# PSUM laid out by engine, seven-row x tiles and one DMA transpose per unit in a fused convolution and expert layer

## The chip, the cores and the metric

The kernel runs on one core of a Trainium2 chip. The metric is the device time of one execution in microseconds, lower is better. Five engines have instruction streams of their own: TensorE (PE, with its weight loads as PEld), VectorE (DVE), ScalarE (ACT), GpSimd (POOL) and SyncE (SP). SP issues most of the DMAs, in the order of its program, and POOL those that scatter rows.

## The reference

For each of 8 batches of 3584 tokens with 192 channels, a causal convolution over 7 taps with weights of its own for every token and head (a softmax over the taps), and then a top-1 layer of 8 experts on all 28672 tokens:

```python
w = softmax(weight_gen)                          # B, S, 8 heads, 7 taps
out = np.einsum('bshk,bskhg->bshg', w, x_unf)    # x_unf: the token and the 6 before it
x = out.reshape(28672, 192)
e_idx = np.argmax(x @ w_gate, axis=1)
gate_w = softmax(x @ w_gate)[e_idx]
eom = sigmoid(x @ w_output_gate)
h = relu(x[mask] @ w1[e])                        # w1: 8 x 192 x 1024
out[mask] = gate_w * eom[e] * (h @ w2[e])        # w2: 8 x 1024 x 192
```

## The kernel before

**Units.** The tokens are cut into 32 units of 896, four to a batch. In a unit a partition holds 7 consecutive tokens (`JS` = 7), so a tile of 7 rows has 7 x 192 = 1344 columns. The causal taps need the 6 rows before (the halo), so an `x` tile holds 13 rows, 2496 columns. `x_load` loads all 13 from DRAM for a unit that is not the first of its batch (24 of the 32); the first of a batch gets zeros from ACT (`zero_steps`) in place of rows before its start.

**The convolution of a unit.** `softmax_steps` makes the tap weights. DVE's share of them, `tw`, goes to PSUM; there are several places for it, among them 3904 and 1344, which lie in banks into which PE writes sums. `tap_steps` then multiplies rows by weights, four or five of the seven taps on POOL (tile `gap`), the rest on DVE. For the first 6 units (`PE_U`) PE adds the products with identity matmuls in f32; from unit 6 on DVE adds them in PSUM (`acc_steps`).

**From sums to tokens in DRAM.** `sum_steps` scales a unit's sum on ACT and splits it into high and low f16 halves on DVE (tile `rt`). The gate needs these rows with channels on partitions (tile `gt`). For units 0 to 4, `pe_logits` turns two rows at a time: six transposes on PE into one place of PSUM, `turn`, then one ACT copy of 128 x 768 (the seventh row alone, 128 x 384), four rounds per unit. From unit 5 on (`TR_U`) SP issues seven DMA transposes per unit, each of three blocks of 128 x 128 f16, 189 in all. Then come logits on PE, softmax, argmax and ranks on DVE, and POOL scatters the rows to their expert's places in `srtd` in DRAM (7 scatters per unit).

**Experts.** In the front, `weight_steps` and `split_steps` load, scale and split the 8 experts' weights and write them to `wd` in DRAM; the sum of squares from which the scale comes is reduced by a matmul in the place that the turned rows use. Tiles of up to 512 tokens of one expert are then formed in rounds. For a tile SP reads its number, then loads `meta`, `xT` (a DMA transpose from `srtd`), `wa` and `wb`; PE runs GEMM1, ACT makes `hh` and DVE `hl` from it (high and low halves), PE runs GEMM2, ACT scales it to `ys`, and POOL scatters it out. The first tile is loaded after the eighth expert has been written.

**Order.** No instruction's place is decided at run time. While the kernel is built, generators ("chains") yield the engine on which they want to issue next, and a planner (`Order`, `Paced` for engines, `Queue` for SP) with a model of costs (`LAT`, `ARRIVE`, `LEAD` and others) picks whose turn it is. A waiting instruction holds everything behind it on its engine. PE's writes and other engines' accesses to PSUM wait for each other by bank of 512 f32 columns, whichever columns of the bank are touched. The tiles are numbered in the order of their loads.

Of the kernel before, what the change touches and what calls it, by code (L numbers as in the profile page):

```python
# [9 lines left out]
F16 = mybir.dt.float16  # L10
# [8 lines left out]
W = 194  # L19
WW = 3585  # L20
# [63 lines left out]
class Order:  # L84


    def __init__(self):
        self.now, self.chains, self.port, self.ring = 0.0, [], 0.0, Ring()
        self.cur = Chain(None, (), 0.0, None)

    def add(self, gen, rank, engine, t=None):
        c = Chain(gen, rank, self.cur.t if t is None else t, engine)
        c.label = label(gen)
        c.favour = FAVOUR.get(c.label, 0.0)
        self.chains.append(c)
        return c

# [42 lines left out]
class Queue:  # L140
# [12 lines left out]
    def __getattr__(self, name):  # L153
        f = getattr(self.engine, name)

        def call(*args, **kwargs):
            c, own, issue = self.order.cur, self.cost(name, args, kwargs), self.issue(name, args, kwargs)
            r = f(*args, **kwargs)  # L158
            if self.host is not None:
                self.issued = max(self.host.t, c.t)  # L160
                self.host.t = self.issued + issue
            self.issued = max(self.issued, self.order.now) + issue
            if own is not None:
                done = self.order.ring.land(self.issued - issue + ARRIVE, own)
                self.moved = max(self.moved, done)
                c.t = max(c.t, done + LANDED)
            return r

        return call


class Paced:
# [8 lines left out]
    def __getattr__(self, name):  # L181
        f = getattr(self.engine, name)

        def call(*args, **kwargs):
            if self.first is not None:
                self.first(self.order.cur.t - self.t)
            c, own = self.order.cur, self.cost(name, args, kwargs)
            r = f(*args, **kwargs)  # L188
            if own is not None:
                held = LOCK and self.holds is not None and self.holds(kwargs)  # L190
# [63 lines left out]
def sync_issue(name, args, kwargs):  # L254
    return 1.29 if name == "dma_start_transpose" else 0.48
# [20 lines left out]
def kernel(ctx: ExitStack, tc: tile.TileContext, x, wg, wgate, wogate, w1, w2, cst, out):  # L276
# [58 lines left out]
    tr_free, lg_free, rk_free, tw_free = [0.0], [(0.0, 2048)], [(0.0, 2272), (0.0, 2288)], []  # L335
# [4 lines left out]
    turn = ps[:, 1536:1920].bitcast(F16)  # L340
# [17 lines left out]
    rest_free = [(0.0, 3904), (0.0, 1344)]  # L358
# [46 lines left out]
    zeros = cp.tile([1, D], F32, name="zeros")  # L405
    nc.gpsimd.memset(zeros, 0.0)
# [15 lines left out]
    for i in range(RT):  # L422
        rt_free.append((0.0, rp.tile([P, JS, W], I32, name=f"rt_{i}")))
# [7 lines left out]
    rr = cf[0:1, o : o + RMAX * 9].rearrange("p (a b) -> p a b", b=9)  # L431
    o += RMAX * 9
# [20 lines left out]
    nc.vector.tensor_copy(f_rr, rr[:, :, 0])  # L453
    pad = cp.tile([P, W], I32, name="pad")
    nc.gpsimd.memset(pad, 0)
    nc.gpsimd.memset(pad[:, 193:194], 65535)
# [58 lines left out]
    def gate_steps():  # L515
# [11 lines left out]
        pg = ps[:, 2304:2320]  # L527
# [34 lines left out]
    def split_steps(e, st1, st2):  # L562
# [7 lines left out]
        yield from take(tr_free, T_)  # L570
        pg = ps[:, 1536:1538]
# [4 lines left out]
        yield from scales(pg[:, 0:2], sc, inv, f"w{e}", tr_free)  # L576
# [37 lines left out]
    def load_steps():  # L614
        for u in range(1, NU):
# [7 lines left out]
            yield from take(x_free, SP)  # L623
            x_load(u)
# [12 lines left out]
    def softmax_steps(u):  # L637
# [20 lines left out]
        if u == PE_U - 1:  # L658
            yield V, lambda: rest_free or tw_free
        home = tw_free if u >= PE_U or (u == PE_U - 1 and not rest_free) else rest_free  # L660
        _, at = yield from take(home, V)
        tw = ps[:, at : at + NV * (K - n)].rearrange("p (v k) -> p v k", k=K - n)
        V.tensor_tensor(out=tw, in0=w4[:, :, n:K], in1=f_mx.unsqueeze(2).broadcast_to([P, NV, K - n]), op=ALU.mult)
        U[u]["tw"], U[u]["tw_at"], U[u]["tw_k"], U[u]["tw_home"] = tw, at, n, home
# [7 lines left out]
    def tap_steps(eng, tag):  # L672

        for u in range(NU):
# [4 lines left out]
            yield eng, lambda: "soft" in d and "zero" in d and (tag == "ga" or "split" in U[u - 2])  # L679
            od.cur.t = max(od.cur.t, d["wt"], d["xt"])  # L680
# [98 lines left out]

    def sum_steps(u):  # L780

        d = U[u]
        _, ri = yield from take(rt_free, S)
        d["ri"], rt = ri, ri.bitcast(F16)
# [22 lines left out]
        if u >= TR_U:  # L807
            yield from take(gt_free, TQ)
            gt = rp.tile([P, JS, 3, P], F16, tag="gt", bufs=GT, name=f"gt{u}")
            for j in range(JS):  # L810
                TQ.dma_start_transpose(out=gt[:, j], in_=rt[:, j, 0:384])
# [9 lines left out]
        else:  # L821
            od.cur.t += LAT_T
            for j0 in range(0, JS, 2):
                yield T_
                for j in range(j0, min(j0 + 2, JS)):
                    logits(lg, j, gt[:, j].rearrange("p k r -> p (k r)"))
            gt_free.append(od.cur.t)

        lz = d["lz"] = sp.tile([P, JS, 3, 8], F32, tag="lz", name=f"lz{u}")
# [10 lines left out]
        eq = sp.tile([P, JS, 8], F32, tag="eq", name=f"eq{u}")  # L840
        mb = m.unsqueeze(2).broadcast_to([P, JS, 8])
        V.tensor_tensor(out=l8, in0=l8, in1=mb, op=ALU.subtract)
        ex = d["ex"] = sp.tile([P, JS, 8], F32, tag="exl", name=f"exl{u}")
# [28 lines left out]
    def pe_logits(u, rt, lg):  # L872

        gx = None
        yield from take(gt_free, S)
        gt = rp.tile([P, JS, 3, P], F16, tag="gt", bufs=GT, name=f"gt{u}").rearrange("p j k r -> p j (k r)")
        for g0 in range(0, JS + 2, 2):
            for g in range(2):
                j = g0 - 2 + g
                if gx is not None and j < JS:  # L880
                    logits(lg, j, gt[:, j])
            ng = min(2, JS - g0)
            if ng > 0:
                yield from take(tr_free, T_)
                pt = turn
                for g in range(ng):
                    for k in range(3):
                        T_.transpose(out=pt[:, g * 384 + k * 128 : g * 384 + (k + 1) * 128], in_=rt[:, g0 + g, k * 128 : (k + 1) * 128], identity=ident)
                yield S
                gx = True  # L890
                S.copy(gt[:, g0 : g0 + ng, 0:384], pt[:, 0 : ng * 384].rearrange("p (j c) -> p j c", c=384))
                tr_free.append(od.cur.t)
                yield T_
        gt_free.append(od.cur.t)
        U[u]["turned"] = True

# [29 lines left out]
    def place_steps(u):  # L926
# [40 lines left out]
        rt_free.append((d["sent_t"], d["ri"]))  # L967
# [226 lines left out]
    def bank_steps():  # L1194
# [4 lines left out]
        yield T_, lambda: any(f[1] == 1344 for f in rest_free)  # L1199
        rest_free.remove(next(f for f in rest_free if f[1] == 1344))  # L1200
        bank_free.extend((got[0], 512 * i) for i in range(3))

    def last_sum_steps():
# [3 lines left out]
        acc_free.append(t)  # L1207
        yield T_, lambda: "all" in state
        bank_free.extend((od.cur.t, at) for at in (2560, 3072, 3584, 2048))

    def last_turn_steps():
# [8 lines left out]
        tw_free.append((t, 2048))  # L1220
# [87 lines left out]
    with tc.For_i(0, left, 1):  # L1308
        first_weights(wp, 1, "more")
        _, more = wa_free.pop()  # L1310
        for to, of in ((f_done, state["done"]), (f_rr, rr[:, :, 0])):
# [36 lines left out]
LAT = 0.118  # L1348
LAT_S = 0.191
LAT_P = 0.34  # L1350
LAT_T = 1.864
LOCK = True
ARRIVE = 1.3
LANDED = 0.8
LAT_R = 1.0
SLACK = 0.024
SCATTER = 0.987
SMALL = 0.066
EAGER = 0, 0.2, (2, 3, 4)
LEAD = 4.586  # L1360
# [15 lines left out]
SHARES = {4: 5, 5: 5, 8: 5, 13: 4, 31: 4}  # L1376
# [9 lines left out]
WBX = 5.532  # L1386
# [25 lines left out]
```

## Time and profile before

| | |
|---|---|
| median of three runs | 1239.97 us (1239.14 to 1242.26) |
| the profiled execution | 1237.59 us, of it 1235.8 us span |
| busy: PE, PEld | 1126.0 us (91%), 816.4 us (66%) |
| busy: DVE, ACT, POOL | 941.5 us (76%), 588.4 us (48%), 834.4 us (68%) |
[...]
| DMA | 291.75 MB, mean 236 GB/s |

The profile is of one execution; a share is of the span. The kernel has four stages in time: a front in which sums, gate and expert weights are made (0 to about 150 us), a stage in which the first tiles run beside units 5 to 10 or so (to about 420 us), a steady stage (to about 1010 us) and a tail with tiles alone. So busy time is read by stage. A wait is given as the engine that waited, the tile it was about to write and what it waited for last. An instruction of SP shows as SPq; its time is how long SP was held, not how long the transfer took.

### The profile page before, as it was taken

The page shows a single profiled execution, that of the slowest core. Times are in us where ns is not written, and L with a number is a line of the kernel's source. Part 1 is how long each engine was busy: PE and PEld are TensorE (multiplying, and loading weights), DVE is VectorE, ACT ScalarE, POOL GpSimd, SP SyncE. Part 2 cuts the span into 40 slices and gives each one's busy share as a digit, 9 for nine tenths or more (in the row PEclk, how much of TensorE's full clock was granted, in tenths as well). Part 3 has the DMA queues.
Part 4 walks back from the last instruction along what each step waited for, and adds up shares of the span by engine and source line. Part 5 has one row for each costly group of instructions (what it writes and reads, how often), then busy time and mean ns, then how long its engine had stood idle before and what let it go on. Part 6 is the DMA issues. An engine that isn't in the chain of part 4 may idle for free.

```text
span 1235.8 us, 27278 instructions
## 1 busy us (share of the span) xinstructions
PE 1126.0 (91%) x9705; PEld 816.4 (66%) x9705; DVE 941.5 (76%) x1874; ACT 588.4 (48%) x1261; POOL 834.4 (68%) x618
## 2 busy tenths in 40 slices
PE   8888896889887899999989999999999999999997
PEld 4444585667555566666666666666666667888987
DVE  6788588878989899999988989999998663333331
ACT  3777353444544445454554545545454433443442
POOL 6457875967767768888878788788788644322222
PEclk9998898899999899999999999999999999999999
DMA  9988796999885898699879877997878597789991
GB/s 309 290 293 286 237 277 191 245 285 249 246 223 135 233 285 210 187 247 265 224 197 256 246 214 219 254 254 225 212 204 211 143 239 214 221 256 299 299 308 53
DMA packets 279402, 291.75 MB, mean 236 GB/s; under 512 B 213670, under 2 KB 238743, under 8 KB 276192
## 3 DMA queue, kind: packets, MB, share of 16 engines
q1 hardware_dynamic: 257424, 245.41, 71.6%
q0 software_dynamic: 21696, 44.30, 13.0%
q8 instruction: 76, 1.25, 0.4%
q14 instruction: 62, 0.51, 0.2%
q10 hardware_dynamic: 144, 0.29, 0.1%
HBM read 189.03 MB, written 60.28 MB: 202 GB/s over the span
## 4 chain that ended last, share of the span: by engine, by line
PE 46%; DVE 25%; DMA 10%; issue 8%; SPq 5%; POOL 2%; ACT 2%; another core or an unknown queue 1%; DVEq 0%; POOLq 0%; ACTq 0%
PE ps L188 46%; DVE ps L188 11%; DVE hl L188 6%; SPq L158 5%; DMA wa<-wd 3%; DVE vt L188 2%; DMA w<-in_wg_dram 2%; DVE rt L188 2%; POOL srtd L188 1%; DMA out_dram<-ys,meta 1%; DMA gt<-rt 1%; ACT rt L188 1%; DMA srtd<-rt,posi 1%; DVE w L188 1%
## 5 line engine op out<-in xcount | busy, mean ns | idle before, releaser
L188 PE MATMUL ps<-xT,wa 128*128 128x512 f16 (+3 forms) x2440 | 494.1, 349 | 58.1 <-DVE hl L188 24.4
L188 PE MATMUL ps<-wb,hh 128*128 128x192 f16 x3648 | 476.2, 248 | 10.9 <-DVE hl L188 4.9
L188 PE MATMUL ps<-wb,hl 128*128 128x192 f16 x1824 | 451.6, 248 | 1.7 <-issue 1.7
L188 DVE SCALAR_TENSOR_TENSOR hl<-ps,hh 128x512 f16<-128x512 f32 (+1 forms) x470 | 306.4, 666 | 183.2 <-ACT hh L188 121.1
L188 POOL TENSOR_TENSOR gap<-x,w 128x1344 f32<-128x1344 f32 x145 | 375.4, 2594 | 47.9 <-PE ps L188 23.9
L188 PEld LDWEIGHTS <-wa 128*128 128x128 f16 x2440 | 227.1, 98 | 245.5 <-issue 54.7
L188 POOL DMA_INDIRECT out_dram<-ys,meta x220 | 218.7, 994 | 242.7 <-ACT ys L188 190.3
L188 PEld LDWEIGHTS <-hh 128*128 128x128 f16 x3648 | 333.6, 98 | 53.3 <-issue 14.4
L188 ACT ACTIVATE hh<-ps 128x512 f16<-128x512 f32 (+1 forms) x470 | 268.2, 582 | 209.0 <-PE ps L188 176.1
L188 POOL DMA_INDIRECT srtd<-rt,posi x224 | 227.6, 1016 | 97.7 <-issue 65.2
L188 ACT ACTIVATE ys<-ps,sc 128x192 f32<-128x192 f32 x228 | 95.8, 420 | 263.7 <-PE ps L188 165.7
L188 DVE TENSOR_TENSOR ps<-ps,gap 128x1344 f32<-128x1344 f32 x121 | 187.7, 1551 | 1.6 <-POOL gap L188 1.1
L188 PEld LDWEIGHTS <-hl 128*128 128x128 f16 x1824 | 179.6, 98 | 5.2 <-issue 4.9
L188 PE MATMUL ps<-gap,cf 128*128 128x512 f32 x144 | 63.1, 578 | 1.9 <-POOL gap L188 1.9
L188 DVE SCALAR_TENSOR_TENSOR rt<-ps,sx,rt 128x448 f16<-128x448 f32 x64 | 57.7, 908 | 9.1 <-ACT rt L188 4.9
L188 DVE TENSOR_TENSOR ps<-ps,vt 128x1344 f32<-128x1344 f32 x35 | 54.4, 1555 | 0.0
L188 DVE TENSOR_TENSOR vt<-x,ps 128x1344 f32<-128x1344 f32 x35 | 54.1, 1545 | 0.2
L188 PE MATMUL ps<-xT,late 128*128 128x128 f16 (+2 forms) x560 | 51.9, 250 | 1.0 <-DMA late<-wd 1.0
L188 ACT ACTIVATE rt<-ps,sx 128x1344 f16<-128x1344 f32 x32 | 44.1, 1379 | 18.2 <-DVE sx L188 13.3
L188 ACT ACTIVATE rt<-ps 128x1344 bf16<-128x1344 f32 x32 | 41.3, 1291 | 21.1 <-issue 13.1
L188 PE MATMUL ps<-vap,cf 128*128 128x512 f32 (+1 forms) x108 | 46.6, 572 | 0.9 <-DVE vap L188 0.9
L188 PEld LDWEIGHTS ps<-gap,cf 128*128 128x128 f32 x144 | 27.5, 202 | 28.6 <-issue 23.3
(120 smaller groups left out, 759.1 us busy)
## 6 DMA issues: line engine op xcount, KB each, us to landing
wb<-wd SPq DMA_DIRECT2D x75, 768.5 KB
wa<-wd SPq DMA_DIRECT2D x61, 768.0 KB
x<-in_x_dram SPq DMA_DIRECT2D x24, 1248.0 KB
late<-wd SPq DMA_DIRECT2D x14, 768.0 KB
wa<-wd SPq DMA_DIRECT2D x61, 128.0 KB
w<-in_wg_dram SPq DMA_DIRECT2D x32, 196.0 KB
wd<-wpb SPq DMA_DIRECT2D x8, 768.5 KB
st<-in_w_dram SPq DMA_DIRECT2D x8, 768.0 KB
```

Of the source, the lines that this page charges most:

```text
L158: r = f(*args, **kwargs)
L188: r = f(*args, **kwargs)
```

## The change

1. *PSUM in the front by engine.* `tw` has one place, 2048, in a bank which only DVE uses, until the sums on PE are done; then 3904 is added. The sums of squares of the experts have a place of their own (1984) and no longer that of the turned rows. Logits, ranks and the gate's sums move within banks. Turned rows have one place of 192 f32 columns: one row at a time, three transposes on PE and one ACT copy of 128 x 384, seven rounds per unit, in chains of their own (`turn_steps`, `copy_steps`). POOL's taps start when its own share of the weights is ready.
2. *The planner* counts waits by bank (`open`, `close`, `banks`), lets a DMA transpose hold SP until 1 us before it is done (`BACK`), and has other constants. The units for which POOL takes a tap more or less are others (`SHARES`); the total stays 145.
3. *x tiles.* The 24 loads fetch 7 rows (1344 columns) instead of 13. The 6 rows of the halo are copied by ACT from the tile of the unit before (`halo_steps`, 128 x 1152 f32). The load of a unit also waits until the tile that it replaces has been copied from.
4. *One DMA transpose per unit.* `rt` has a row pitch of 256 words, so one DMA transpose turns 27 blocks of 128 x 128 (`NB`; the fourth block of each row is padding), where seven turned 21.

```diff
+RW = 256
...
+    def open(self, engine, args, kwargs):
+
+        t, out = 0.0, kwargs.get("out", args[0] if args else None)
+        for o in (*args, *kwargs.values()):
+            for b in banks(o):
+                for log in (self.wrote[b], self.read[b]) if o is out else (self.wrote[b],):
+                    t = max(t, *(v for e, v in log.items() if e is not engine), 0.0)
+        return t
...
+                if name == "dma_start_transpose":
+                    self.issued = max(self.issued, done - BACK)
...
-    tr_free, lg_free, rk_free, tw_free = [0.0], [(0.0, 2048)], [(0.0, 2272), (0.0, 2288)], []
+    pg_free, lg_free, rk_free, tw_free = [0.0], [(0.0, 1728)], [(0.0, 1952), (0.0, 1968)], [(0.0, 2048)]
...
-    turn = ps[:, 1536:1920].bitcast(F16)
+    tr_free = [(0.0, ps[:, at : at + 192].bitcast(F16)) for at in TURNS]
...
-    rest_free = [(0.0, 3904), (0.0, 1344)]
...
-            U[u]["zero"] = True
-            SP.dma_start(out=loads[u], in_=xb[:, q * JS - HALO : (q + 1) * JS, :])
+            od.add(halo_steps(u), (RANK_H, u), S, U[u - 1]["xt"])
+            SP.dma_start(out=loads[u][:, HALO:, :], in_=xb[:, q * JS : (q + 1) * JS, :])
+
+    def halo_steps(u):
+        S.activation(loads[u][:, 0:HALO, :], loads[u - 1][:, JS : JS + HALO, :], AF.Copy)
...
-        yield from take(tr_free, T_)
-        pg = ps[:, 1536:1538]
+        yield from take(pg_free, T_)
+        pg = ps[:, 1984:1986]
...
+            if u >= XN:
+                yield SP, lambda: "zero" in U[u - XN + 1]
             x_load(u)
...
-            gt = rp.tile([P, JS, 3, P], F16, tag="gt", bufs=GT, name=f"gt{u}")
-            for j in range(JS):
-                TQ.dma_start_transpose(out=gt[:, j], in_=rt[:, j, 0:384])
+            gt = rp.tile([P, NB, P], F16, tag="gt", bufs=GT, name=f"gt{u}")
+            TQ.dma_start_transpose(out=gt, in_=d["flat"].bitcast(F16)[:, 0 : NB * P])
...
+    def turn_steps(u, rt, gt, copied):
+        for j in range(JS):
+            _, pt = yield from take(tr_free, T_)
+            for k in range(3):
+                T_.transpose(out=pt[:, k * 128 : (k + 1) * 128], in_=rt[:, j, k * 128 : (k + 1) * 128], identity=ident)
+            od.add(copy_steps(gt[:, j], pt, copied, j), (RANK_B, u), S, T_.t + LAT_P)
+
+    def copy_steps(to, pt, copied, j):
+        S.copy(to, pt)
+        tr_free.append((od.cur.t, pt))
...
-LAT = 0.118
-LAT_S = 0.191
+LAT = 0.0756
+LAT_S = 0.2324
...
-ARRIVE = 1.3
-LANDED = 0.8
+ARRIVE = 1.9478
+LANDED = 0.5447
...
-LEAD = 4.586
+LEAD = 3.3869
...
+BACK = 1.0
+TURNS = (1536,)
...
-SHARES = {4: 5, 5: 5, 8: 5, 13: 4, 31: 4}
+SHARES = {18: 5, 11: 4, 28: 4, 20: 4}
...
-WBX = 5.532
+WBX = 3.3548
```

What this does to the order is shown at three places of SP's program. In the rows, a number after a name is that of its unit or tile; TENSOR_LOAD reads the number of a tile's expert, and the ISA rows prepare the DMA that follows.

The first place is the end of the front, before:

```order
L158 DMA wd_79<-wa1_143 64x256 x6
L158 DMA wd_79<-wpb7_1206 128x1537
L158 TENSOR_LOAD ti2_0_1041
L158 ISA x2
L1100 ISA
L158 DMA meta0_1329<-srtd_78 128x2x2
L158 ISA
L158 DMA_TRANSPOSE xT0_1331<-srtd_78 128x3x256
```

and now:

```order
L175 DMA wd_79<-wpb7_1223 128x1537
L175 DMA w8_1303<-in_wg_dram 128x392
L175 DMA x8_1314<-in_x_dram 112x1152
L175 DMA x8_1314<-in_x_dram 15x1152
L175 DMA x8_1314<-in_x_dram 128x1344
L175 TENSOR_LOAD ti2_0_1071
L175 ISA x2
L1144 ISA
L175 DMA meta0_1381<-srtd_78 128x2x2
L175 ISA
L175 DMA_TRANSPOSE xT0_1383<-srtd_78 128x3x256
```

The loads of unit 8 stood behind tile 2 and now stand between the eighth expert's write and tile 0.

The second place is around the turned rows of unit 5, before:

```order
L158 DMA wb3_1617<-wd_79 128x1537
L158 DMA_TRANSPOSE gt5_1742<-rt_2_101 128x3x128 x7
L158 DMA yd0_1877<-ys0_1640 128x384
L158 TENSOR_LOAD ti2_0_1041
L158 ISA x2
L1100 ISA
L158 DMA meta4_1892<-srtd_78 128x2x2
```

and now:

```order
L175 DMA wb2_1499<-wd_79 128x1537
L175 DMA_TRANSPOSE gt5_1590<-rt_2_104 128x27x128
L175 TENSOR_LOAD ti2_0_1071
L175 ISA x2
L1144 ISA
L175 DMA meta3_1717<-srtd_78 128x2x2
L175 ISA
L175 DMA_TRANSPOSE xT3_1719<-srtd_78 128x3x256
```

They stood between tiles 3 and 4 and now stand between tiles 2 and 3. Those of unit 6 stand ahead of tile 5 in both.

The third place is around tile 16, before:

```order
L158 DMA w15_4713<-in_wg_dram 128x392
L158 DMA x15_4715<-in_x_dram 128x2496
L158 DMA_TRANSPOSE gt12_4883<-rt_0_99 128x3x128 x7
L158 TENSOR_LOAD ti10_0_4532
L158 ISA x2
L1100 ISA
L158 DMA meta16_5036<-srtd_78 128x4x2
L158 ISA
L158 DMA_TRANSPOSE xT16_5038<-srtd_78 128x3x512
```

and now:

```order
L175 DMA x15_4701<-in_x_dram 128x1344
L175 TENSOR_LOAD ti10_0_4530
L175 ISA x2
L1144 ISA
L175 DMA meta16_4886<-srtd_78 128x4x2
L175 ISA
L175 DMA_TRANSPOSE xT16_4888<-srtd_78 128x3x512
L175 ISA
L175 DMA wa0_142<-wd_79 128x1536
```

The turned rows of unit 12 stood ahead of tile 16 and now stand behind its last load.

## Rows read from the trace of the kernel before

**Rows 1.** By stage: length; PE, PEld, DVE, ACT, POOL busy; clock, DMA share, GB/s.

```profile
0.00:150.00 150.00, 128.04 (x569) 70.06 (x570) 112.34 (x237) 92.72 (x151) 99.05 (x65) 0.94 0.89 282
150.00:420.00 270.00, 224.72 (x1991) 168.71 (x1989) 227.53 (x467) 122.68 (x284) 197.72 (x139) 0.94 0.88 237
420.00:1010.00 590.00, 557.41 (x4810) 393.83 (x4808) 529.04 (x1049) 285.53 (x644) 471.17 (x346) 0.99 0.84 224
1010.00:1236.00 226.00, 215.84 (x2343) 183.82 (x2340) 72.62 (x122) 87.45 (x183) 66.50 (x70) 0.99 0.82 235
```

**Rows 2.** Waits of PE, 150 to 420 us: total us, times, longest.

```profile
PE ps L188 <- DMA wa<-wd: 23.1, 4, 8.1
PE ps L188 <- DVE hl L188: 13.0, 15, 2.8
```

**Rows 3.** Waits of PE, 420 to 1010 us, its two largest.

```profile
PE ps L188 <- DVE hl L188: 16.3, 28, 1.9
PE ps L188 <- issue: 7.5, 15, 1.0
```

**Rows 4.** Timeline of PE: start, us, operation, idle before and its releaser.

```profile
192.76 1.46 PE L188 MATMUL ps<-xT,wa 128*128 128x256 f16 x6 [6.36 <-DMA wa<-wd]
...
219.54 1.78 PE L188 MATMUL ps<-xT,wa 128*128 128x384 f16 x5 [7.02 <-DMA wa<-wd]
...
406.13 2.31 PE L188 MATMUL ps<-xT,wa 128*128 128x512 f16 x5 [8.06 <-DMA wa<-wd]
```

**Rows 5.** Timeline of SP's queue around tile 16: start, us, operation, count.

```profile
386.05 9.82 SPq L158 DMA_TRANSPOSE gt<-rt  x7
398.39 0.00 SPq L158 DMA_DIRECT2D meta<-srtd  x1
398.44 1.46 SPq L158 DMA_TRANSPOSE xT<-srtd  x1
```

**Rows 6.** Timeline of POOL: the last scatter of unit 10.

```profile
384.84 0.98 POOL L188 DMA_INDIRECT srtd<-rt,posi  x1 [0.30 <-issue]
```

**Rows 7.** Timeline of SP's queue from the eighth expert's write to tile 5.

```profile
140.46 0.34 SPq L158 DMA_DIRECT2D wd<-wpb  x1
142.32 0.42 SPq L158 DMA_DIRECT2D meta<-srtd  x1
142.89 1.33 SPq L158 DMA_TRANSPOSE xT<-srtd  x1
...
158.12 3.84 SPq L158 DMA_DIRECT2D x<-in_x_dram  x3
...
170.63 11.53 SPq L158 DMA_TRANSPOSE gt<-rt  x7
...
184.26 0.40 SPq L158 DMA_DIRECT2D meta<-srtd  x1
...
198.04 9.73 SPq L158 DMA_TRANSPOSE gt<-rt  x7
...
211.24 0.41 SPq L158 DMA_DIRECT2D meta<-srtd  x1
```

**Rows 8.** Operations of SP's line: ns min/median/max, first and last start.

```profile
L158 SPq DMA_TRANSPOSE gt<-rt x189: 1183/1256/3902, 170.6 to 986.3; - x189
...
L158 SPq DMA_TRANSPOSE xT<-srtd x75: 925/1494/7698, 142.9 to 1198.3; - x75
```

**Rows 9.** Busy time by stretch, after the wait before tile 16.

```profile
395.00:405.00 10.00, 3.06 (x30) 2.31 (x27) 9.93 (x11) 1.98 (x5) 7.81 (x7) 0.77 0.72 180
405.00:410.00 5.00, 3.87 (x29) 1.75 (x30) 2.44 (x4) 1.49 (x3) 1.66 (x2) 0.50 1.13 270
```

**Rows 10.** Groups of instructions: busy us, mean ns, idle before.

```profile
L188 ACT ACTIVATE x<-zeros 1x1152 f32<-1x1152 f32 x8 | 9.2, 1148 | 0.0
```

**Rows 11.** Instructions on tile gt: ns min/median/max.

```profile
L188 ACT COPY gt<-ps x20: 479/784/799, 42.2 to 154.2; 128x768 f16<-128x768 f16 x15, 128x384 f16<-128x384 f16 x5
```

**Rows 12.** Waits in the front, 0 to 150 us: total us, times, longest.

```profile
ACT gt L188 <- PE ps L188: 16.2, 11, 4.0
...
PE ps L188 <- DVE w L188: 3.2, 2, 1.7
...
PE ps L188 <- DVE winv L188: 1.7, 1, 1.7
```

**Rows 13.** Instructions on tile xT: count, ns, first and last start.

```profile
L188 PE MATMUL ps<-xT,wa x2440: 219/379/634, 152.6 to 1209.5; 128*128 128x512 f16 x127, 128*128 128x256 f16 x25, 128*128 128x384 f16 x21, 128*128 128x128 f16 x15
```

More of the change, by code (lines that the diff above doesn't have):

```diff
@@ L88, in __init__ @@
         self.now, self.chains, self.port, self.ring = 0.0, [], 0.0, Ring()
+        self.wrote, self.read = [{} for _ in range(8)], [{} for _ in range(8)]
         self.cur = Chain(None, (), 0.0, None)
@@ L96, in add, with close @@
         return c
+    def open(self, engine, args, kwargs):
[5 more added lines that the diff above has]
+        return t
+    def close(self, engine, args, kwargs, t):
+        out = kwargs.get("out", args[0] if args else None)
+        for o in (*args, *kwargs.values()):
+            for b in banks(o):
+                (self.wrote if o is out else self.read)[b][engine] = t
     def named(self, text):
@@ L200, in call, with banks @@
                 c.t = max(c.t, self.t + self.after)
+                self.order.close(self, args, kwargs, self.t + (LAT_P if self.after == 0.0 else self.after))
             return r
         return call
+def banks(o):
+    if getattr(o, "space", None) != bass.MemoryType.PSUM:
+        return ()
+    size = 2 if o.dtype in (F16, BF16) else 4
+    lo = o.offset % (16384 // size)
+    hi = lo + sum(st * (n - 1) for st, n in o.ap[1:])
+    return range(lo * size // 2048, hi * size // 2048 + 1)
 def two_in_sbuf(kwargs):
@@ L403, in zero_steps @@
         yield
-    zeros = cp.tile([1, D], F32, name="zeros")
-    nc.gpsimd.memset(zeros, 0.0)
+    pad = cp.tile([P, W], I32, name="pad")
+    nc.gpsimd.memset(pad, 0)
+    nc.gpsimd.memset(pad[:, 193:194], 65535)
+    zeros = pad[:, 0:D].bitcast(F32)
     w_free.pop()
@@ L430 @@
     o = 256
[L431 to L432 removed]
+    rr = cf[0:1, o : o + RMAX]
+    o += RMAX
     need = {}
@@ L452 @@
     nc.vector.memset(f_z[:, 8, :], float(DUMMY))
[L453 to L456, printed above, removed]
+    nc.vector.tensor_copy(f_rr, rr)
     segs = cp.tile([P, 8 * JS], F16, name="segs")
@@ L575, in split_steps @@
         inv = sp.tile([P, 2], F32, tag="winv", name=f"winv{e}")
-        yield from scales(pg[:, 0:2], sc, inv, f"w{e}", tr_free)
+        yield from scales(pg[:, 0:2], sc, inv, f"w{e}", pg_free)
         s1, s2 = sc[:, 0:1], sc[:, 1:2]
@@ L657, in softmax_steps @@
         yield V
[L658 to L661, printed above, removed]
+        U[u]["gw"], U[u]["pool"] = od.cur.t, True
+        _, at = yield from take(tw_free, V)
         tw = ps[:, at : at + NV * (K - n)].rearrange("p (v k) -> p v k", k=K - n)
         V.tensor_tensor(out=tw, in0=w4[:, :, n:K], in1=f_mx.unsqueeze(2).broadcast_to([P, NV, K - n]), op=ALU.mult)
-        U[u]["tw"], U[u]["tw_at"], U[u]["tw_k"], U[u]["tw_home"] = tw, at, n, home
+        U[u]["tw"], U[u]["tw_at"], U[u]["tw_k"] = tw, at, n
         mx_free.append(od.cur.t)
@@ L778, in add_steps, with rows_of @@
             od.add(sum_steps(u), (RANK_B, u), S, T_.t + LAT_P)
+    NB = 4 * JS - 1
+    def rows_of(flat):
+        return bass.AP(flat.tensor, flat.offset, [flat.ap[0], [RW, JS], [1, W]])
     def sum_steps(u):
         d = U[u]
-        _, ri = yield from take(rt_free, S)
-        d["ri"], rt = ri, ri.bitcast(F16)
+        _, flat = yield from take(rt_free, S)
+        ri = rows_of(flat)
+        d["flat"], d["ri"], rt = flat, ri, ri.bitcast(F16)
         ssq = sp.tile([P, 1], F32, tag="ssq", name=f"ssq{u}")
@@ L872, in pe_logits @@
     def pe_logits(u, rt, lg):
-        gx = None
         yield from take(gt_free, S)
[L876 to L893, printed above, removed]
+        gt = rp.tile([P, NB, P], F16, tag="gt", bufs=GT, name=f"gt{u}")[:, 0 : 3 * JS].rearrange("p (j k) r -> p j (k r)", k=3)
+        copied = {}
+        od.add(turn_steps(u, rt, gt, copied), (RANK_B, u), T_)
+        for j in range(JS):
+            yield T_, lambda: j in copied
+            od.cur.t = max(od.cur.t, copied[j])
+            logits(lg, j, gt[:, j])
         gt_free.append(od.cur.t)
         U[u]["turned"] = True
+    def turn_steps(u, rt, gt, copied):
+        for j in range(JS):
+            _, pt = yield from take(tr_free, T_)
[5 more added lines that the diff above has]
+        tr_free.append((od.cur.t, pt))
+        copied[j] = od.cur.t
+        return
+        yield
     def exp_steps(u, ex, l8):
```

47 lines of the change are left out of this document (25 added, 22 removed).

## The prediction

> **What bounds the kernel now.** I read the table by stage first [rows 1]. Its columns are busy time, so a stage's length less PE's busy time is what PE loses there: 22.0 us in the first 150 us (the front), 45.3 between 150 and 420, 32.6 between 420 and 1010, 10.2 in the tail. PE is the bound from 150 on, at 83, 94 and 96% of a stage. In the front nothing is full: PE 85%, DVE 75%, POOL 66%, ACT 62%; it ends when the eighth expert is written and a chain of small steps has run. DVE is at 90% between 420 and 1010 and will matter if PE gets quicker.
>
> The waits of PE come second. Between 150 and 420 four waits for the load of `wa` make 23.1 us and the waits for `hl` 13.0 [rows 2]; between 420 and 1010 the largest is `hl` with 16.3, and `wa` is none of those listed [rows 3]. So what a tile's loads cost is paid in the first third only. Three of the four waits stand in [rows 4], 6.36, 7.02 and 8.06 us; the first, at 177 us, is the rest of 23.1, 1.7.
>
> Third, I asked why those loads came late, on SP's queue. For the tile whose GEMM starts at 406.13 SP stands in the seven `gt` transposes of unit 12 from 386.05 for 9.82 us and issues `meta` at 398.39 [rows 5]. Its tokens had been there long before: POOL ended the last scatter of unit 10 at 384.84 + 0.98 = 385.8 [rows 6]. That is 12.6 us in which the load could have gone out. The same shape stands twice earlier [rows 7]: the transposes of unit 5 hold SP for 11.53 us from 170.63 and `meta` follows at 184.26; those of unit 6 hold it for 9.73 from 198.04 and `meta` follows at 211.24. PE's waits are thus SP's order and SP's holding time, as long as tokens are ahead.
>
> **The change part by part.**
>
> *One transpose for seven.* Of 189 small transposes one holds SP for 1.256 us in the median [rows 8], so seven cost 8.8 and, with what stood between, 9.7 to 11.5 [rows 5, 7]. No row shows a transpose of 27 blocks. The order rows give blocks of 128 by 128: 3 for a small `gt`, 6 for `xT` of tile 0 (3 by 256 rows), 12 for `xT` of tile 16 (3 by 512). They held SP for 1.256, 1.33 and 1.46 us [rows 5, 7, 8], 0.02 a block, so 27 blocks would hold it for about 1.46 + 15 x 0.022 = 1.8. Against that, an `xT` has held SP for as much as 7.70 [rows 8], where earlier transfers were still under way. I take 4 us, nearer the flat rows than the longest one; the ends are 1.8 and 12.6 (below). SP is so freed some 6 us per unit of 27. Most of it buys nothing: PE does not wait for loads after 420 [rows 3].
>
> [...]
>
> *SP's order.* Tile 16 moves ahead of `gt12`. It would be issued from about 386 to 389, and 7.7 us from `meta` to the first matmul (406.13 - 398.39) put that at about 397, where PE ran dry (406.13 - 8.06 = 398.07). The whole 8.06 goes. Tile 5 stays behind `gt6` and gains that transpose's 5.7 us (9.73 - 4): 7.02 becomes 1.3. Tile 4 stays behind `gt5` and gains 7.5 (11.53 - 4): 6.36 becomes 0. The 1.7 of tile 3 stays; it moves behind `gt5` (+4) and loses the loads of unit 8 ahead of it (-4, [rows 7]). That leaves 3 of the 23.1. But a tile that comes earlier finds its tokens, its weight buffer and `hl` less ready; I leave 8 and book **-15**, ends -8 (tile 16 alone) and -20.
>
> *Clock.* [...] Four gaps, two of them as long: **-3**, ends 0 and -6.
>
> *x tiles and halo.* A unit that isn't the first of its batch loads 1344 instead of 2496 columns, 576 KB less in each of 24 loads. The 16 DMA engines are busy 82 to 89% [rows 1], and the larger transpose takes part of it back; no wait of the path is for x, so I book 0. In exchange ACT copies 128 x 1152 once per such unit. One partition of that length took 1.148 us [rows 10], and I take the same for 128. From 420 on that is 18 copies, 20.7 us of ACT's 304 idle. Each can stand ahead of a `hh` that DVE's `hl` and then PE wait for [rows 3]. All in the path would be +20.7, none 0; ACT being free half the time, and PE being reached only through 28 `hl` waits in 18 units, I book **+2**.
>
> *The front.* Four things. The loads of unit 8 now stand ahead of tile 0: 3.84 us on SP [rows 7], of which the 1.5 us between the issue of the eighth expert's write (140.46 + 0.34) and tile 0's `meta` (142.32) may cover most: **+2.5** on the first GEMM. ACT has 6 halo copies more before the last weights (6.9 us) and 23 copies of one row's transposes at 0.479 instead of 12 of two at 0.784 [rows 11], +1.6: together 8.5 on an engine with 57 idle. I put a third on the path, **+3**. Turned rows go through PE, ACT, PE seven times for a unit and not four, and their PSUM place waits for the copy: ACT's 11 waits for PE before such copies were 16.2 us, 1.5 each [rows 12]. At most 15 more rounds would stand in the path, 22 us; logits run beside the next unit's taps, so I book 0 and keep 22 as a rival. For it, waits that were only for a bank go: PE for DVE's weights `w` 3.2 and for `winv` 1.7 [rows 12], **-5**, and the weight scales no longer share the turn place. The front so comes out at +0.5, from -7 to +11.
>
> *The tail* keeps its work: 0. The two planner parts (bank waits, new constants) act only through the order above.
>
> Sum: -15 - 3 + 2 + 0.5 = -15.5. The profiled execution took 1237.59, so 1222.1; the median of the three runs is 2.4 above it, and I predict **1225 us**.
>
> **Rivals.**
> 1. *Tokens become the bound.* PE gets its 18 us between 150 and 420 and waits for them later, since DVE is at 90% from 420 on [rows 1] and the units' sums come no sooner. For it: that 90%. Against it: DVE's program is interleaved with `hl`, so an earlier PE also moves DVE. Only the 3 us of the clock stay: 1240 - 3 = 1237.
> 2. *Slower: the front's round trips.* One turn place, 35 rounds where there were 20, and halo copies in front of them on ACT. If the 15 more rounds cost 1.5 us each [rows 12] where the eighth expert's scales or the first tiles' scatter wait, the first GEMM at 152.6 [rows 13] moves by 22: 1225 + 22 = 1247. It decides once the first GEMM comes after about 168. Against it: ACT 62% and PE 85% busy [rows 1].
> [...]
> 4. *More than forecast.* Nothing comes in place of the four waits (-20) and the front shortens by its -7 instead of +0.5: 1225 - 5 - 7.5 = 1212.
>
> **How the numbers follow.** Chances: forecast 0.46, rival 1 0.12, rival 2 0.17, rival 3 0.12, rival 4 0.13. A change under 0.3% (3.7 us) can't be told from none in this kernel. The forecast's own range, 1216 to 1234, and rival 4 are faster, as are a half of rival 1 and of rival 3 (1237 and 1236.5 lie at the bound of 1236.3): 0.46 + 0.13 + 0.12 = 0.71. The other halves make the same, 0.12. Slower is rival 2: 0.17. The range leaves out half of rival 2 and a third of rival 4: 1209 to 1246.
>
> **What would show it.** Right: a `gt` row of 27 with a median near 4 us; PE's `wa` waits between 150 and 420 under 10 us; no stretch like 395 to 405 before tile 16; first GEMM between 146 and 163; the stage from 420 on as long as before. Wrong: a `gt` hold near 10 us (rival 3), a first GEMM after 168 with longer waits of ACT's copies for PE (rival 2), or new waits of PE for loads whose scatter has just landed, from 420 on (rival 1).

## The result and the profile after

The changed kernel took 1224.19 us in the median of four runs (1220.87 to 1225.7), the kernel before 1239.56 beside it (1233.86 to 1242.26): a ratio of 0.988, with a 95% interval of 0.984 to 0.992. The prediction was 1225. The profiled execution took 1223.71 us, 13.9 less than the one of before, with a span of 1222.0.

The view by stage of the changed kernel answers to [rows 1], with the same columns:

```profile
0.00:150.00 150.00, 124.84 (x583) 68.38 (x583) 126.11 (x239) 102.96 (x176) 109.70 (x68) 0.98 0.85 266
150.00:420.00 270.00, 239.31 (x2156) 180.58 (x2157) 247.19 (x496) 135.06 (x310) 210.64 (x147) 0.95 0.91 238
420.00:1010.00 590.00, 555.63 (x4756) 390.82 (x4754) 518.85 (x1048) 298.07 (x647) 463.09 (x348) 0.99 0.87 222
1010.00:1222.00 212.00, 200.20 (x2203) 172.32 (x2200) 63.76 (x93) 80.54 (x169) 58.12 (x60) 0.99 0.78 226
```

Between 150 and 420 PE now does 239.31 us of work where it did 224.72. But a stage that is cut by the clock compares different work. So I counted PE's GEMM matmuls in order, which are 8472 in both kernels, and cut where the same number has been issued. The table gives the length of each piece and how PE spent it, in us ("other" is sums, turned rows, logits and the like):

```
GEMM matmuls      before: length gemm other idle    after: length gemm other idle    length
start to first            152.6   0.0 130.8  22.0           151.3   0.0 124.8  26.5    -1.3
0 to 600                   91.2  67.9   4.4  18.9            92.3  71.7   2.6  18.2    +1.1
600 to 1800               180.7 151.3   3.1  26.3           159.0 144.7   3.4  11.0   -21.7
1800 to 6000              569.3 524.0  12.8  32.6           570.6 526.4  12.4  31.8    +1.3
6000 to last              234.0 231.2   0.6   2.2           241.1 233.3   0.6   7.3    +7.1
```

Each piece holds the same number of matmuls of each shape in both kernels. The front gives 1.3, the first 600 matmuls (to about 244 us) nothing, the next 1200 (to 403) 21.7; the steady stage keeps that, and the tail gives 7.1 back.

PE's waits between 150 and 420 answer to [rows 2]:

```profile
PE ps L207 <- DMA wa<-wd: 11.6, 4, 5.7
PE ps L207 <- issue: 8.8, 12, 1.8
PE ps L207 <- DVE hl L207: 4.5, 6, 1.5
PE ps L207 <- DVE p L207: 3.5, 1, 3.5
PE ps L207 <- DVE ez L207: 3.1, 1, 3.1
```

The waits for `wa` fell by 11.5, those for `hl` by 8.5 (13.0 to 4.5), and two waits that were not in the list before, for `p` and `ez`, take 6.6. They stand in the first 600 matmuls, where `issue` also rose, from 1.8 to 7.0. What is left of the waits for `wa` stands in new places: 4.74 us before the very first GEMM, where PE before ran 4.31 us of padding matmuls instead, and 5.68 at 348.89:

```profile
151.32 1.03 PE L207 MATMUL ps<-xT,wa 128*128 128x256 f16 x4 [4.74 <-DMA wa<-wd]
...
348.89 1.46 PE L207 MATMUL ps<-xT,wa 128*128 128x512 f16 x3 [5.68 <-DMA wa<-wd]
```

So in the 1200 matmuls that give the 21.7, most of the gain is not in `wa`. PE's three largest waits there, before (243.8 to 424.5 us) and after (243.6 to 402.6):

```profile
PE ps L188 <- DVE hl L188: 10.8, 13, 2.8
PE ps L188 <- DMA wa<-wd: 8.1, 1, 8.1
PE ps L188 <- issue: 6.0, 12, 1.0
```

```profile
PE ps L207 <- DMA wa<-wd: 5.7, 1, 5.7
PE ps L207 <- DVE hl L207: 2.4, 4, 0.8
PE ps L207 <- issue: 1.6, 3, 0.8
```

Around tile 16, SP's queue answers to [rows 5], and POOL's last scatter of unit 10 to [rows 6]:

```profile
374.98 0.40 SPq L175 DMA_DIRECT2D meta<-srtd  x1
375.53 1.48 SPq L175 DMA_TRANSPOSE xT<-srtd  x1
377.34 1.04 SPq L175 DMA_DIRECT2D wa<-wd  x2
378.63 0.38 SPq L175 DMA_DIRECT2D wb<-wd  x1
379.17 8.92 SPq L175 DMA_TRANSPOSE gt<-rt  x1
```

```profile
372.31 0.98 POOL L207 DMA_INDIRECT srtd<-rt,posi  x1 [0.30 <-issue]
```

`meta` goes out 1.7 us after the scatter ended (372.31 + 0.98 = 373.29), not 12.6. The transpose of unit 12 stands behind the tile's loads and holds SP for 8.92 us, more than twice what was forecast. The instructions on tile `gt` answer to [rows 8, 11]:

```profile
L207 ACT COPY gt<-ps x35: 452/473/487, 41.1 to 155.8; 128x384 f16<-128x384 f16 x35
L175 SPq DMA_TRANSPOSE gt<-rt x27: 4327/8002/10403, 159.0 to 969.5; - x27
```

In the tail, SP's queue and PE stand so:

```profile
1131.12 0.40 SPq L175 DMA_DIRECT2D meta<-srtd  x1
1131.72 8.50 SPq L175 DMA_TRANSPOSE xT<-srtd  x1
1140.43 1.11 SPq L175 DMA_DIRECT2D late<-wd  x2
```

```profile
1146.44 3.41 PE L207 MATMUL ps<-xT,late 128*128 128x512 f16 x10 [3.67 <-DMA late<-wd]
```

This is a tile of 512 tokens among small ones. Its `xT` holds SP for 8.50 us, and only then are its weights asked for; PE waits 3.67 us, where no wait of the tail before was over 1. Two tiles of 512 stood among the small ones before, too; their `xT` held SP for 6.04 and 6.27 us, and PE waited 0.98 for one and not for the other.

### The profile page after: what moved, and what is told of

Its sections match the earlier page's. It is cut to its first block, busy times and chain, and to the rows that moved or that the text cites. A ratio compares the mean times of both kernels' runs of the same rounds, so it can differ in the third digit from the quotient of the medians.

```text
span 1222.0 us, 27128 instructions
## 1 busy us (share of the span) xinstructions
PE 1120.0 (92%) x9693; PEld 812.1 (66%) x9693; DVE 955.9 (78%) x1874; ACT 616.6 (50%) x1300; POOL 841.5 (69%) x620
## 3 DMA queue, kind: packets, MB, share of 16 engines
q0 software_dynamic: 21696, 44.30, 12.5%
## 4 chain that ended last, share of the span: by engine, by line
PE 58%; DVE 17%; DMA 9%; issue 8%; POOL 5%; ACT 1%; SPq 1%; another core or an unknown queue 0%; POOLq 0%; DVEq 0%; ACTq 0%
PE ps L207 58%; DVE ps L207 9%; DVE hl L207 4%; DMA wa<-wd 4%; POOL srtd L207 3%; DMA srtd<-rt,posi 2%; POOL gap L207 1%; DVE vt L207 1%; SPq L175 1%; DMA gt<-rt 1%; DMA meta<-srtd 1%; DVE rt L207 1%; POOL out_dram L207 1%; DVE lz L207 1%; DMA w<-in_wg_dram 1%
## 5 line engine op out<-in xcount | busy, mean ns | idle before, releaser
L207 POOL TENSOR_TENSOR gap<-x,w 128x1344 f32<-128x1344 f32 x145 | 379.4, 2624 | 43.2 <-issue 14.8
L207 POOL DMA_INDIRECT srtd<-rt,posi x224 | 230.2, 1028 | 85.2 <-issue 57.8
L207 PE MATMUL ps<-xT,late 128*128 128x128 f16 (+2 forms) x560 | 59.9, 263 | 3.7 <-DMA late<-wd 3.7
L207 PEld LDWEIGHTS <-late 128*128 128x128 f16 x560 | 40.2, 98 | 16.5 <-DMA late<-wd 3.9
L207 ACT ACTIVATE rt<-ps,sx 128x1344 f16<-128x1344 f32 x32 | 44.2, 1380 | 11.4 <-DVE sx L207 8.2
L207 PE MATMUL ps<-gm,gt 128*128 128x32 f16 x672 | 28.1, 177 | 20.1 <-ACT gt L207 10.4
```

## The experiments

Every kernel ran beside the kernel before on its own chip. The chips differ: the kernel before took 1239.6 where the result was measured, 1202.5 on the chip of a_same to a_oldplan, 1232.0 on that of micro to a_psum and 1203.8 on that of the last four. What makes them differ was not looked into. So ratios to the kernel before are compared, and times only on one chip. In three kernels (a_seven, a_x13 and b_one) the accounting of the planner was kept as it was and only what is issued was changed, so the order of every engine's program is the one of the kernel that they start from; in their edits `parts` is what is issued in place of what the planner accounts for, and `ghost` accounts for an instruction that isn't issued.

**a_same.** The changed kernel, nothing edited.

> The changed kernel once more, as the measure for the three kernels that each undo one part of it. Both theories: 1221 to 1226 us, PE's waits for wa between 150 and 420 near 12 us, a gt row of 27 with a median near 8.0 us, and the tail giving back some 6 of the 20 us that stand at 1010.

Measured: 1182.91 us, ratio 0.983 (0.981 to 0.986), a median hold of 7.64 us. The waits for `wa` were 21.1, not 12: on this chip they are as long as those of the kernel before on the first, and the kernel is still 20 us faster than its neighbour. So the sum of these waits is not by itself where the gain sits. The tail takes 241.0 us again.

**a_seven.** Seven transposes again, in the order of the changed kernel:

```diff
-TQ.dma_start_transpose(out=gt, in_=d["flat"].bitcast(F16)[:, 0 : NB * P])
+each = [(gt[:, 4 * j : 4 * j + 3], rt[:, j, 0:384]) for j in range(JS)]
+TQ.dma_start_transpose(out=gt, in_=d["flat"].bitcast(F16)[:, 0 : NB * P], parts=each)
```

> The changed kernel with seven DMA transposes of three blocks per unit in place of one of 27, every engine's program otherwise in the order of the changed kernel. Theory 1, that the time came from a shorter hold of SP: the hold goes back from 8.0 to about 9.8 us, and each of the tiles that stand behind a gt in the first third (tiles 3, 5, 17) comes 2 us later, so 3 to 8 us slower, 1227 to 1232. Theory 2, that the time came from the order (loads issued ahead of the transposes) and not from the hold: 0 to 2 us slower, 1224 to 1226.

Measured: 1185.96 us, 3.0 slower than a_same; the two intervals overlap (ratio 0.987, 0.985 to 0.990). That lies at the edge between the two theories. In this order the single transpose is worth little. It moves more than that inside the run: by matmuls a_seven takes 10.0 us longer than a_same from 1800 to 6000 and 8.4 less in the tail (232.6). PE's largest wait after 1010, for the loads of a late tile (`late`), is 1.1 us in a_seven and 3.2 in a_same.

**a_x13.** The 13-row loads, without the copies on ACT:

```diff
-SP.dma_start(out=loads[u][:, HALO:, :], in_=xb[:, q * JS : (q + 1) * JS, :])
+whole = [(loads[u], xb[:, q * JS - HALO : (q + 1) * JS, :])]
+SP.dma_start(out=loads[u][:, HALO:, :], in_=xb[:, q * JS : (q + 1) * JS, :], parts=whole)
...
-S.activation(loads[u][:, 0:HALO, :], loads[u - 1][:, JS : JS + HALO, :], AF.Copy)
+S.activation(loads[u][:, 0:HALO, :], loads[u - 1][:, JS : JS + HALO, :], AF.Copy, ghost=True)
```

> The changed kernel with the 13-row x loads of before and no halo copies on ACT, every engine's program otherwise in the same order. Theory 1, that the DMA queue is what makes loads and transposes slow: 576 KB more in 24 units, the median hold of gt rises from 8.0 to 9 us or more, 2 to 6 us slower. Theory 2, that the halo copies on ACT cost more than the bytes save: 1 to 4 us faster, since 24 copies of 1.16 us are gone from ACT.

Measured: 1190.97 us, 8.1 slower than a_same, ratio 0.992 (0.989 to 0.995). Theory 2 is out: the copies cost less than the bytes. Theory 1 has the sign; the time was above its range and the hold below it. The median hold rose to 8.50 us, and PE's largest wait from 420 to 1010 is for `gt`, here in a_x13:

```profile
PE ps L213 <- DMA gt<-rt: 12.3, 6, 4.2
```

and in a_same:

```profile
PE ps L207 <- DMA gt<-rt: 6.5, 4, 2.8
```

**a_oldplan.** The planner of before in the changed kernel:

```diff
 def open(self, engine, args, kwargs):
+    return 0.0
...
-LAT = 0.0756
+LAT = 0.118
...
-BACK = 1.0
+BACK = 1000.0
...
-SHARES = {18: 5, 11: 4, 28: 4, 20: 4}
+SHARES = {4: 5, 5: 5, 8: 5, 13: 4, 31: 4}
```

> The changed kernel with the planner of before: no bank waits counted, no hold of SP by a transpose, the old constants and the old units for POOL's fifth tap; the PSUM places, seven-row x tiles and the single transpose stay. Theory 1, that the parts themselves carry the gain: 1222 to 1229. Theory 2, that the new order carries it: 1233 to 1241, with waits of PE for wa of 20 us or more between 150 and 420.

Measured: 1193.59 us, 10.7 slower than a_same, ratio 0.993 (0.990 to 0.995). As ratios to 1239.56, theory 1 was 0.986 to 0.991 and theory 2 0.995 to 1.001, so the result lies between the two. As theory 2 has it the order matters, but it leaves a kernel that is still faster than before. Between 150 and 420 the waits for `wa` are 21.6 (a_same 21.1), those for `hl` 11.4 (a_same 4.0). The transposes, placed elsewhere, hold SP for a median of 4.78 us:

```profile
L176 SPq DMA_TRANSPOSE gt<-rt x27: 4084/4780/12016, 171.0 to 939.6; - x27
```

**micro.** The hold by itself.

```diff
+for n, k in ((1, 3), (1, 6), (1, 12), (1, 21), (1, 27), (7, 3)):
+    turn(n, k, f"q{r}_{n}x{k}")      # empty queues
...
+    load()                           # two loads of 128 x 2496 f32
+    turn(n, k, f"l{r}_{n}x{k}")
```

> Nothing of the computation is left in it: transposes alone, from one SBUF tile, one after another, each of 3, 6, 12, 21 or 27 blocks or seven of 3, twice with empty DMA queues and twice right behind two loads of 1248 KB; the output is a copy of x. Theory 1, that SP is held for the transfer and for what is queued ahead of it: with empty queues 27 blocks hold SP 4.0 to 4.8 us, 21 some 3.3, 12 some 2, 3 about 1.2, and behind the loads 27 blocks hold it 3 us longer or more, while the hold of seven of 3 grows less, being 7 times 1.2 us of issuing. Theory 2, that SP's time is one push per block of its own, whatever is queued: the hold of 27 is the same, 8 us, in both places.

Measured, on the timeline of SP's queue: 3, 6, 12, 21 and 27 blocks with empty queues, then seven of 3; and behind the loads 3, 21 and 27 blocks (`l_1x`) and seven of 3 (`l_7x`):

```profile
7.84 1.29 SPq L41 DMA_TRANSPOSE q_1x<-src  x1
10.62 1.21 SPq L41 DMA_TRANSPOSE q_1x<-src  x1
13.70 1.27 SPq L41 DMA_TRANSPOSE q_1x<-src  x1
17.70 3.23 SPq L41 DMA_TRANSPOSE q_1x<-src  x1
23.01 4.04 SPq L41 DMA_TRANSPOSE q_1x<-src  x1
29.22 8.97 SPq L41 DMA_TRANSPOSE q_7x<-src  x7
...
76.85 1.21 SPq L41 DMA_TRANSPOSE l_1x<-src  x1
...
86.84 9.43 SPq L41 DMA_TRANSPOSE l_1x<-src  x1
...
99.82 9.76 SPq L41 DMA_TRANSPOSE l_1x<-src  x1
...
112.97 10.99 SPq L41 DMA_TRANSPOSE l_7x<-src  x7
```

Theory 2 is out, and theory 1 holds for the large transposes alone. 27 blocks take 4.04 us in empty queues and 9.76 behind 2.5 MB of loads, while seven of 3 take 8.97 and 10.99. But up to 12 blocks the hold in empty queues is flat (some 2 us were expected for 12), and 3 blocks right behind the same loads are held for 1.21 us, no longer than without them. Where between 12 and 21 blocks the growth begins, and what makes it, these runs do not show. So one transpose saves 4.9 us here with empty queues (8.97 to 4.04) and 1.2 behind the loads (10.99 to 9.76). In the changed kernel the same split can be seen by how long before a transpose SP issued its last large load:

```
us since the load    transposes    hold in us: median (min to max)
under 2                      17    8.83 (7.23 to 10.40)
2 to 6                        4    6.41 (5.39 to 6.76)
over 6                        6    4.83 (4.33 to 5.03)
```

**b_same** and **b_one.** The kernel before, and the kernel before with one transpose in its own order:

```diff
-for j in range(JS):
-    TQ.dma_start_transpose(out=gt[:, j], in_=rt[:, j, 0:384])
+for j in range(JS):
+    one = [] if j else [(gt, d["flat"].bitcast(F16)[:, 0 : NB * P])]
+    TQ.dma_start_transpose(out=gt[:, 4 * j : 4 * j + 3], in_=rt[:, j, 0:384], parts=one)
```

> The kernel before once more, for a profile on the chip of the experiments: PE's waits for wa between 150 and 420 of 15 to 25 us, and the tiles behind the transposes 8.8 us or more later.

> The kernel before with one DMA transpose of 27 blocks in place of seven, in the order of before (and the smaller constants that make room for the padded rows). Theory 1, that a shorter hold of SP is worth little, since what is issued earlier queues in the DMA engines: 0 to 4 us faster than before. Theory 2, that the hold kept tiles 4, 5 and 16 waiting: 5 to 12 us faster, the four waits for wa (23.1 us) down to 12 or less.

Measured: b_same 1234.18 us in its one run; b_one 1218.37, ratio 0.987 (0.984 to 0.989). This part alone, in the order of before, gives 13.7 us, near what the whole change gave on the first chip. That is above the range of theory 2, but the waits for `wa` fall from 24.1 only to 16.7, not to 12. Three rows of PE in b_same and the same tiles (4, 5 and 16) in b_one:

```profile
195.84 1.46 PE L188 MATMUL ps<-xT,wa 128*128 128x256 f16 x6 [5.64 <-DMA wa<-wd]
...
224.36 2.10 PE L188 MATMUL ps<-xT,wa 128*128 128x384 f16 x6 [8.72 <-DMA wa<-wd]
...
409.96 1.46 PE L188 MATMUL ps<-xT,wa 128*128 128x512 f16 x3 [7.56 <-DMA wa<-wd]
```

```profile
194.19 2.10 PE L194 MATMUL ps<-xT,wa 128*128 128x256 f16 x9 [5.20 <-DMA wa<-wd]
...
219.92 2.42 PE L194 MATMUL ps<-xT,wa 128*128 128x384 f16 x7 [7.38 <-DMA wa<-wd]
...
395.38 1.25 PE L194 MATMUL ps<-xT,wa 128*128 128x512 f16 x5 [2.63 <-DMA wa<-wd]
```

Tiles 4 and 5 still wait; tile 16 waits 4.9 less. That answers to how long SP was held ahead of each. Ahead of tile 16 (unit 12) it is, in b_same and in b_one:

```profile
390.39 9.56 SPq L158 DMA_TRANSPOSE gt<-rt  x7
```

```profile
380.74 4.71 SPq L164 DMA_TRANSPOSE gt<-rt  x1
```

Here theory 2 holds: 4.85 less of holding, 4.9 less of waiting. Ahead of tile 4, right behind loads, the hold only falls from 10.52 to 9.71. Ahead of tile 5 it falls from 9.82 to 4.09, but two small DMAs between it and the tile (`yd`) then hold SP for 5.53 where they held it for 3.30, and the tile waits 1.3 less. Counted by matmuls, b_one takes 12.0 us off the pieces from 0 to 1800 (9.8 of it idle time, of which 7.4 are these waits for `wa`), 3.5 off the steady stage, and gives 2.4 back in the tail.

**a_psum.** The PSUM places and turned rows alone; a_oldplan's edit and two more, with the order planned anew:

```diff
+for j in range(JS):
+    TQ.dma_start_transpose(out=gt[:, 4 * j : 4 * j + 3], in_=rt[:, j, 0:384])
...
-od.add(halo_steps(u), (RANK_H, u), S, U[u - 1]["xt"])
...
+U[u]["zero"] = True
+SP.dma_start(out=loads[u], in_=xb[:, q * JS - HALO : (q + 1) * JS, :])
```

> The changed kernel with all other parts undone: seven transposes, 13-row x loads, the planner of before; only the PSUM places, the turned rows by ones and the small tiles remain, and the order follows from them. Undone one at a time the three others cost 3.0, 8.1 and 10.7 us of 19.6; if they add, 2 us slower than before to 2 faster. If the PSUM layout carries a part of its own that the others hide: 4 us faster or more. If its 35 round trips cost: 4 us slower or more.

Measured: 1231.21 us, ratio 0.999 (0.997 to 1.001). The layout by itself changes nothing in the whole time that can be measured, in either direction. Inside the run it does: in the one profile of each, its first GEMM comes 4.4 us before that of b_same (151.3 against 155.7) and the stretch from 0 to 1800 matmuls is 9.8 shorter, and from 1800 to 6000 it takes 11.5 more, with waits for `hl` of 25.5 from 420 to 1010 (11.9 in b_same), and 5.1 more in the tail. There a gain in the first third is lost again, in the way of rival 1, though in waits for `hl` and not for tokens.

**a_ctl** and **b_newplan.** The changed kernel for the third time, and the kernel before with the new planner alone (the functions `open`, `close` and `banks`, `BACK` and all the constants of the diff).

> The changed kernel a third time, as the measure for the two that change one of its numbers. It has been 0.988 and 0.983 of the kernel before on two chips; a third ratio between these.

> The kernel before with the new planner alone (bank waits counted, the hold of a transpose, the new constants and units of POOL's fifth tap); seven transposes, 13-row loads and the PSUM places of before stay. Theory 1, that the new order is good by itself, as undoing it in the changed kernel cost 10.7 us: 0.988 to 0.993 of before. Theory 2, that it and the single transpose take away the same waits, and that with seven transposes it has little to gain: 0.996 to 1.004.

Measured: a_ctl 1182.94 us, ratio 0.981 (0.977 to 0.985). b_newplan 1228.32, ratio 1.020 (1.016 to 1.023): 24.5 us slower than before. Both theories fall. One place carries most of it; PE and SP's queue there:

```profile
363.24 2.31 PE L207 MATMUL ps<-xT,wa 128*128 128x512 f16 x5 [21.08 <-DMA wa<-wd]
```

```profile
344.12 8.97 SPq L175 DMA_TRANSPOSE gt<-rt  x7
354.75 0.41 SPq L175 DMA_DIRECT2D meta<-srtd  x1
```

The planner puts the transposes ahead of a tile that is already wanted: SP waits 7.9 us there for the rows to be turned, the seven hold it for 8.97, and PE runs dry for 21 us. Why it places them so was not looked into. The same numbers, in a kernel for which they were not made, cost more than they gave there.

**a_turn2.** A second place for turned rows:

```diff
-TURNS = (1536,)
+TURNS = (1536, 1344)
```

> The changed kernel with a second place for turned rows (1344, in the bank of the first sum), so that PE can turn the next row while ACT copies; the order is planned anew. If the one place is what makes PE wait 10.4 us for ACT's copies in the front and that delays the end: first GEMM 2 to 5 us earlier and 2 to 5 us faster. If the round trips lie beside other work: within 2 us of the changed kernel, with the waits for copies down.

Measured: 1177.25 us, 5.7 faster than a_ctl (ratio 0.976, 0.972 to 0.980, which overlaps a_ctl's), and the first GEMM at 144.1 instead of 151.8. PE's waits for the copies, 7.9 us up to 150 in a_ctl, are 0.9. But the place lies in the bank in which PE still adds up a unit's sum, and this kernel no longer computes the same output, so the routing may differ too and the time is only an indication. What alters the output no run here shows, and a second place in a bank without a sum was not tried.

**a_latt.** Logits planned later:

```diff
-LAT_T = 1.8143
+LAT_T = 4.0
```

> The changed kernel with the planner's time from a transpose to its logits raised from 1.8 to 4.0 us, since PE waited for gt to land (2.3 us on one chip, 7.1 on the other). If these waits are on the path: they vanish and it is 2 to 6 us faster. If the logits then come late for ranks and scatters: 0 to 5 us slower.

Measured: 1171.24 us, ratio 0.972 (0.968 to 0.975), 11.7 faster than a_ctl and the fastest of all. PE's largest waits from 420 to 1010, in a_ctl:

```profile
PE ps L207 <- DMA gt<-rt: 9.1, 4, 3.4
PE ps L207 <- DVE hl L207: 5.5, 12, 0.9
PE ps L207 <- DMA wa<-wd: 2.0, 1, 2.0
```

and all of them in a_latt:

```profile
PE ps L207 <- DVE hl L207: 4.7, 10, 1.4
```

The waits for `gt` vanish, as expected; the gain is twice the most that was expected. By matmuls a_latt loses 8.9 up to 1800 (one wait for `wa` of 12.6 where a_ctl has 7.2), then wins 12.5 in the steady stage and 6.7 in the tail. In the steady stage the waits that are gone (9.1 us) fit most of the 12.5. But the one number moves the whole order, which was not taken apart: that another order alone gives as much is not ruled out, and what moved the tail is open.

## Why the prediction was right, and where it was not

The total was right to a microsecond, in part by luck. By the table the pieces sum to -13.5, where -15.5 was booked; the first 1800 matmuls gave 20.6 where 18 was booked, and in part from other waits than those named, and the tail took 7.1 back where nothing was booked. Of the five signs that were to show it right, three came (the first GEMM, no such stretch before tile 16, the stage from 420 on); the median hold (8.0, not 4) and the waits for `wa` (11.6, not under 10) did not. By its terms:

- *The stretch from 0 to 1800 matmuls*: -15 of waits and -3 of clock were booked. PE's idle time fell by 16.0 (18.9 + 26.3 to 18.2 + 11.0) and the same GEMM work took 2.8 less (219.2 to 216.4 us, as the granted clock rose from 0.94 to 0.95 between 150 and 420: 3.8 more in the first 600, 6.6 less after them). Both sizes hold, but the places do not. No run shows the -3 of clock by itself, which was the author's estimate. What the traces show is a granted clock that, read by half microseconds, stands at 0.50 for 31.5 us between 150 and 420 before (10 of them from 400.5 to 410.5) and for 18 after (6.5 from 345.5 to 352).
- *Tile 16*: right, place and size. Its loads go out 1.7 us after the scatter, the 8.06 us are gone, and no stretch like that of [rows 9] is left there. What the prediction did not have is the new wait of 5.68 at 348.89, with a clock of 0.54 from 345 to 350. The `meta` of that tile goes out at 340.89, after SP has waited 3.6 us for a scatter (`srtd`): there PE waits for a tile whose tokens have just come. Of the 8.1 us for `wa` from 600 to 1800, 5.7 are still there.
- *Tiles 4 and 5*: this step failed. Their 12 us were to come from a shorter hold, but the first 600 matmuls are 1.1 us longer. The hold was sized at 4 us; it is 8.0. Four is right for empty queues (micro 4.04), and a transpose behind a tile's loads takes 8.8 (a median of 17). Those of units 5 and 6 held SP for 9.09 and 6.76. In the changed kernel the waits for the loads of these tiles did go, but waits for `ez`, `p` and `issue` came in the same place, and PE got no further. b_one shows the single transpose in the order of before: there both waits for loads stay.
- *What made up for it*: the waits for `hl`, which the prediction left alone between 150 and 420, fell by 8.5, and `issue` by 4.4 from 600 to 1800. a_oldplan points to the planner's order (`hl` 11.4 against 4.0 on one chip), but a_psum has 7.2 with the planner of before where b_same has 8.8, so the order alone is not shown to be the cause. The prediction said that the two planner parts act only through the order, and then priced only the three places of SP's.
- *Steady stage*: +2 booked, +1.3 measured.
- *Front*: +0.5 booked, -1.3 measured. The terms inside are not settled. PE did wait longer for ACT's copies, as rival 2 had it: 10.4 us against the 1.6 before, in the list of waits up to 150. a_turn2 suggests that about 7 us of the first GEMM's time hang on the one place. PE's wait of 4.74 for `wa` before the first GEMM, where it ran padding before, lies here too, in the place for which the prediction booked +2.5 for the loads of unit 8. What paid for these I can't say by parts; a_psum, with layout and turned rows alone, has its first GEMM 4.4 earlier than b_same.
- *Tail*: 0 booked, +7.1 measured: 5.1 of idle time and 2.1 of slower matmuls. The tail keeps its work, but not its order, and I read the order only in the first third. The order by itself is not the cause, though: a_seven has the same one, and its tail takes 232.6 us where that of a_same takes 241.0. What makes the loss is open; in a_seven PE reaches the tail 8.4 us later than in a_same and loses that much less in it.

Of the rivals, none came. The third stands nearest, in which SP's hold grows in proportion to the blocks, from 9.8 us for 21 to 9.8 x 27/21 = 12.6 for 27. That was the author's estimate, and no run shows it: in empty queues 27 blocks take 4.04 us, and right behind 2.5 MB of loads 9.76, 5.7 more (micro); in the changed kernel they take 8.83 in the median of the 17 that follow a load within 2 us. A growth with the blocks there is, from 1.27 us for 12 to 4.04 for 27, and its cause is open; from 3 to 12 there is none (1.29, 1.21 and 1.27).

Undone alone in the changed kernel, the parts are worth 3.0 (transposes), 8.1 (x tiles) and 10.7 (planner), together 21.8, near the 19.6 of the whole on that chip; with all three undone (a_psum) nothing is left. In this direction they about add. Added alone to the kernel before they do not: the transpose is worth 13.7 and the planner -24.5. At tile 16 the order and the hold act on the same wait: the order of the changed kernel puts that tile ahead of the transpose, so that its length no longer matters to it, and in the order of before a shorter hold takes 4.9 us off.

## What to carry to other kernels

The hold of an issuing queue had two prices here: a transpose of 27 blocks held SP for 4.04 us with empty queues and for 9.76 behind loads (micro), in the changed kernel for 4.83 in the median where the last large load was over 6 us back and for 8.83 where it was under 2. For 3 blocks there was one (1.29 and 1.21). The place in the program decided which was paid: read what was issued in the 2 us before. In a kernel whose order is planned from a table of costs, parts are worth what they are worth in that order; a part undone alone and a part added alone can differ by 10 us, so try both before a share of the gain is given to one. And when an order changes, follow it to the tail: a gain in the first third was here cut by a third in the last tiles, and in a_psum it was gone by the end.

## What was not expected of the hardware

With empty queues a DMA transpose of 12 blocks held SP no longer than one of 3 in micro (1.27 and 1.29 us), one of 21 took 3.23 and one of 27 4.04; behind 2.5 MB of loads 27 took 9.76 and 21 took 9.43, but 3 only 1.21. And one program differed by 3% between chips: the kernel before took 1202 to 1240 us in the medians of four chips, the changed one 1183 to 1224 on three of them.
